# Beginning the row loads of two granules earlier in a fused attention and MLP kernel

## The chip, the cores and the metric

The kernel runs on one core of a Trainium2 chip. The metric is the device time of one execution, in microseconds (us). A trace gives a span that is some 1.8 us shorter, from the first to the last instruction on the engines. Ratios are the mean time of one kernel's fast runs over that of the other's fast runs of the same rounds, so they are not quite the ratio of the medians quoted beside them. The interval after a ratio is the 95% one.

## The reference, cut to what matters

```python
# attention: 4 batches, 8 heads, 768 positions, head size 64
scores = scale * q @ k^T + bias              # 8 global keys, 96 local keys, slopes by head
x = softmax(scores) @ v                      # then (3072 tokens, 512)
# MLP
h = x @ w_in                                 # 512 -> 2048
g = s * relu(h)**2 + b
out = g @ w_out                              # 2048 -> 512
```

## The kernel before

The 3072 tokens are cut into twelve granules of 256. A granule's k, q and v rows are loaded by GpSimd's DMA queue, which also casts them to bf16. Its k and q are transposed by DMA on SyncE's queue, its attention is computed, the result `xn` is transposed to `xT` by DMA (from granule 4 on), and the MLP follows one granule behind.

The parts that matter here:

```python
def load_granule(j):                 # six DMAs of 128 KB
    load_rows(j, "k"); load_rows(j, "q"); load_v(j)

def pace(j):                         # a one-element copy: GpSimd waits here for t
    t = pts[j, 0][0:1, 0, 0:1] if j < 5 else xT[j - 1][0:1, KC - 1, GT - 1 : GT]
    nc.gpsimd.tensor_copy(pdum[:], t)

def XT_dma(j):                       # two transposes by DMA, SyncE's queue
    xT[j] = xpool.tile([P, KC, GT], BF16, name="xT", tag="xT")
    for i in range(GB):
        nc.sync.dma_start_transpose(xT[j][:, :, i * P : (i + 1) * P], ...xn[j][:, i]...)

def idle(n, tag="pso", cols=4 * P):  # warm-up matmuls on constants
    ...
idle(9, "av")                        # the first work of the TensorE

def period(j, items, at, late=None, mid=()):      # granules 3 and 4
    SS(j, (0, 1))                    # scores, exp, mask product of two head pairs
    if j + 2 < NJ:
        pace(j)
        load_granule(j + 2)          # granules 5 and 6
    ...
    A(j, 0) ; A(j, 1, "psh")
    SS(j, (2, 3))
    A(j, 2) ; KO(j + 1) ; A(j, 3, "psh")   # KO, VO: VectorE copies of k and v
    if late is None:
        XT_dma(j)
    VO(j + 1)
    XB(j + 2)                        # transposes of k and q by DMA
    ...
# granules 5 to 11 (steady): the first product with w_in needs xT of the granule before
```

## Time and profile before

| | before |
|---|---|
| median of 3 runs | 209.95 us (209.49 to 210.19) |
| TensorE busy | 199.7 of 207.9 us |
| TensorE wait for xT of granule 4 | 0.57 us, at 79.36 |
| xT transposes of granule 4, issue to landing | 4.9 and 4.1 us |
| pacing copies for granules 5 and 6 | 54.80 and 66.40 us |

The TensorE's program order fixes what can be won: only where it waits. "SPq" in the views is SyncE's sequencer, which issues a transpose; "x2" is the number of instructions merged in a line; the bracket at the end of a line gives the idle time ahead of it and what ended it.

### The profile page before, as it was taken

To read this page: it belongs to the slowest core of one execution; us is meant where nothing else is said; L and a number is where in the kernel's file an instruction comes from. 1 tells how busy PE (TensorE), PEld (TensorE's weight loads), DVE (VectorE), ACT (ScalarE), POOL (GpSimd) and SP (SyncE) were. 2 spreads that over 40 slices of the span, in tenths; PEclk is the share of its full clock that TensorE was granted. 3 is DMA by queue.
4 is the path that set the end of the run, shared out by engine and by line. 5 is a ranking of instruction groups with operands and counts; after the bars stand their busy time and mean duration, and the time that the engine had idled before them with its cause. 6 is when DMAs were issued, how large, how long until landed. Compare 5 with 4: busy or idle time off the path is not lost.

```text
span 207.9 us, 5589 instructions
## 1 busy us (share of the span) xinstructions
PE 199.7 (96%) x2283; PEld 160.6 (77%) x2292; DVE 166.5 (80%) x401; ACT 120.2 (58%) x184; POOL 74.2 (36%) x98
## 2 busy tenths in 40 slices
PE   7989999999999998999999999999999999999992
PEld 2567976457666777888888988988988988988881
DVE  3575567599889898788799799788799799886682
ACT  5679899445978784636536536536446456425300
POOL 8985673930372806509119109027000000000000
PEclk9999999999999999999999999999999999999999
DMA  6999999999899995999999999969946040040022
GB/s 164 193 183 197 190 196 191 181 144 158 90 121 122 256 161 83 182 120 139 205 113 99 214 98 114 207 101 123 197 79 176 3 151 4 1 151 3 0 106 101
DMA packets 103850, 27.64 MB, mean 133 GB/s; under 512 B 91408, under 2 KB 101904, under 8 KB 103824
## 3 DMA queue, kind: packets, MB, share of 16 engines
q0 software_dynamic: 70976, 13.11, 80.2%
q1 hardware_dynamic: 31792, 13.64, 34.5%
q10 hardware_dynamic: 1056, 0.52, 0.9%
q8 instruction: 18, 0.29, 0.6%
q14 instruction: 8, 0.07, 0.2%
HBM read 27.26 MB, written 6.29 MB: 161 GB/s over the span
## 4 chain that ended last, share of the span: by engine, by line
PE 82%; ACT 9%; DMA 4%; DVE 2%; issue 1%; SPq 0%; ACTq 0%
PE ps L529 36%; PE ps_w L691 15%; PE ps_wb L691 7%; PE ps L590 6%; PE ps_av L447 5%; PE ps_s L396 4%; PE ps_wa L691 3%; ACT pt L409 3%; ACT gT L539 2%; DMA xT<-xn 2%; DMA raw<-in_k_dram 2%; PE ps_2s L590 2%; PE ps_s L380 1%; ACT gT L547 1%; ACT tmpl L256 1%
## 5 line engine op out<-in xcount | busy, mean ns | idle before, releaser
L529 PE MATMUL ps<-xT,w_in_bf 128*128 128x256 bf16 x768 | 96.7, 273 | 1.2 <-DMA xT<-xn 0.6
L529 PEld LDWEIGHTS <-w_in_bf 128*128 128x128 bf16 x768 | 72.8, 98 | 12.4 <-issue 0.9
L541 ACT ACTIVATE gT<-ps 128x512 bf16<-128x512 f32 x72 | 43.0, 598 | 58.7 <-PE ps L529 56.1
L409 ACT ACTIVATE pt<-ps_s 128x1024 bf16<-128x1024 f32 (+1 forms) x48 | 43.0, 951 | 2.7 <-PE ps_s L396 2.6
L691 PEld LDWEIGHTS <-sw 128*128 128x128 bf16 x288 | 28.1, 98 | 3.4
L419 DVE TENSOR_TENSOR pt<-pt,tmpl 128x1024 bf16<-128x1024 bf16 (+1 forms) x40 | 25.2, 648 | 3.0 <-ACT pt L409 2.4
L557 DVE TENSOR_TENSOR gT<-gT 128x512 bf16<-128x512 bf16 x66 | 25.1, 416 | 1.8 <-ACT gT L541 1.6
L691 PEld LDWEIGHTS <-gT 128*128 128x128 bf16 x216 | 20.5, 98 | 3.3 <-issue 0.2
L112 POOL DMA_DIRECT2D vaug<-in_v_dram x24 | 21.5, 912 | 4.2 <-DMA w_out_bf<-in_moe_w_out_dram 1.7
L465 DVE TENSOR_TENSOR xn<-ps_av,rc 128x256 bf16<-128x256 f32 x48 | 20.4, 425 | 1.7
L590 PE MATMUL ps<-w_out_bf,gT 128*128 128x512 bf16 x74 | 18.8, 379 | 0.5 <-issue 0.3
L126 POOL COPY pdum<-xT 1x1 bf16<-1x1 bf16 x5 | 3.8, 758 | 42.0 <-DMA xT<-xn 42.0
L691 PE MATMUL ps_w<-tw,sw 128*128 128x256 bf16 x144 | 18.7, 272 | 0.0
L701 DVE SCALAR_TENSOR_TENSOR u<-ps_w,s_bc,bvec 128x256 f32<-128x256 f32 x27 | 13.0, 480 | 6.7 <-PE ps_w L691 6.7
L447 PEld LDWEIGHTS <-pt 128*128 128x128 bf16 x352 | 15.5, 98 | 3.4 <-DVE xn L465 1.0
L104 POOL DMA_DIRECT2D qnat<-in_q_dram x18 | 16.0, 905 | 2.7 <-PE ps L529 1.4
L447 PE MATMUL ps_av<-vaug,pt 128*128 128x65 bf16 x224 | 16.4, 193 | 0.5 <-DVE xn L465 0.2
L539 ACT ACTIVATE gT<-ps 128x512 bf16<-128x512 f32 x24 | 14.2, 598 | 4.4 <-PE ps L529 4.4
L464 DVE RECIPROCAL rc<-ps_av 128x4 f32<-128x4 f32 x48 | 8.6, 179 | 10.2 <-PE ps_av L447 10.0
L104 POOL DMA_DIRECT2D knat<-in_k_dram x18 | 15.8, 887 | 1.6 <-issue 1.6
L590 PEld LDWEIGHTS <-gT 128*128 128x128 bf16 x96 | 8.6, 98 | 8.2
L396 PE MATMUL ps_s<-qT,kT 64*128 64x128 bf16 x224 | 12.3, 218 | 0.0
(94 smaller groups left out, 238.6 us busy)
## 6 DMA issues: line engine op xcount, KB each, us to landing
out_dram<-o_pr SPq DMA_DIRECT2D x8, 512.0 KB, 4.3
vaug<-in_v_dram POOLq DMA_DIRECT2D x24, 128.0 KB, 7.3
knat<-in_k_dram POOLq DMA_DIRECT2D x22, 128.0 KB, 5.2
qnat<-in_q_dram POOLq DMA_DIRECT2D x22, 128.0 KB, 6.5
w_in_bf<-in_moe_w_in_dram POOLq DMA_DIRECT2D x8, 256.0 KB, 8.3
w_out_bf<-in_moe_w_out_dram POOLq DMA_DIRECT2D x4, 512.0 KB, 10.0
out_dram<-o_pr SPq DMA_DIRECT2D x7, 256.0 KB, 4.0
raw<-in_q_dram ACTq DMA_DIRECT2D x2, 256.0 KB, 5.0
```

Of the source, the lines that this page charges most:

```text
L104: nc.gpsimd.dma_start(t[:, i, :, :], src[b, :, sb * P : (sb + 1) * P, :].rearrange("h p d -> p h d"))
L112: nc.gpsimd.dma_start(vaug[b % 2][:, sb, :, 0:D], v[b, :, sb * P : (sb + 1) * P, :].rearrange("h p d -> p h d"),)
L396: nc.tensor.matmul(ps[:, hi, oc * P : (oc + 1) * P], lhsT=kt[r, :], rhs=qT[j][r, hp, i * P : (i + 1) * P], start=not biased, stop=not bias ...
L409: nc.scalar.activation(pt[:, :, 0:n], ps[:, :, 0:n], ACT.Exp, scale=QSCALE)
L419: nc.vector.tensor_tensor(pt[:, :, 0:n], pt[:, :, 0:n], m, ALU.mult)
L447: nc.tensor.matmul(av[:, i, hi, :], lhsT=pt[:, hi, c * P : (c + 1) * P], rhs=vv, start=n_ == 0, stop=n_ == len(ops) - 1,)
L465: nc.vector.tensor_tensor(xn[j][:, :, 2 * hp : 2 * hp + 2, :], av[:, :, :, 0:D], rc[:].to_broadcast((P, GB, 2, D)), ALU.mult,)
L529: nc.tensor.matmul(ps[:, i, :], lhsT=w_in_bf[:, kc, fc * P : (fc + 1) * P], rhs=xT[j][:, kc, :], start=(kc == 0), stop=(kc == KC - 1),)
L541: nc.scalar.activation(gs.rearrange("p f (r t) -> p f r t", r=2), ps[:].rearrange("p f (t r) -> p f r t", r=2), ACT.Relu,)
L557: nc.vector.tensor_tensor(gs, gs, gs, ALU.mult)
L590: nc.tensor.matmul(po[j, tb], lhsT=gT[j][:, fc, tb * P : (tb + 1) * P], rhs=w_out_bf[:, fc, :], start=(fc == 0), stop=(fc == FC - 1),)
L691: nc.tensor.matmul(wt[j, ps], lhsT=lhs[:, f, :], rhs=rhs[:, f, :], start=first and f == 0, stop=f == HF - 1, skip_group_check=True,)
```

## The change

The intent is to fill a hole in the DMA traffic and get the rows out of the way of later transposes. Granule 5's load moves to the first evacuated output of granule 1, granule 6's to granule 3's third exp.

```diff
-    def pace(j):
-        t = pts[j, 0][0:1, 0, 0:1] if j < 5 else xT[j - 1][0:1, KC - 1, GT - 1 : GT]
+    def pace(t):
         nc.gpsimd.tensor_copy(pdum[:], t)
...
     P2_raw(1, 0)
+    pace(raw[1, 0][0:1, 0:1])
+    load_granule(5)
...
     def period(j, items, at, late=None, mid=()):
         SS(j, (0, 1))
-        if j + 2 < NJ:
-            pace(j)
-            load_granule(j + 2)
...
         SS(j, (2, 3))
+        if j == 3:
+            pace(pts[j, 2][0:1, 0, 0:1])
+            load_granule(6)
...
-            pace(j)
+            pace(xT[j - 1][0:1, KC - 1, GT - 1 : GT])       # granules 7 to 11: as before
             load_granule(j + 2)
```

## The prediction

> **What bounds the kernel now.** I read four views: the engines' busy shares, the waits of the TensorE, the timelines of the three engines around the moved loads, and the DMA share in one-microsecond windows. The busy shares come first, because they say how much there is to win at all.
>
> ```profile
> span 207.9 us, 5589 instructions
> PE 199.7 (96%) x2283; PEld 160.6 (77%) x2292; DVE 166.5 (80%) x401; ACT 120.2 (58%) x184; POOL 74.2 (36%) x98
> ```
>
> The TensorE is busy for 199.7 of 207.9 us, at a granted clock of 1.000 throughout. The loads themselves are on no engine that is full: GpSimd, which issues them, is at 36%. So the change cannot save more than the TensorE waits that these loads cause, and the next view lists those:
>
> ```profile
> PE ps_i L239 <- PEq L1134: 0.8, 1, 0.8
> PE ps L529 <- DMA xT<-xn: 0.6, 1, 0.6
> PE ps_t L272 <- ACT knat L160: 0.6, 1, 0.6
> PE ps L590 <- issue: 0.3, 2, 0.2
> ```
>
> The columns are total us, times, longest. Only the second line is a wait for a transfer: once in the whole run, 0.6 us long, for a transpose by DMA of the attention output. The first and third lie in the first six microseconds, before anything that is changed. The timeline of the TensorE places it:
>
> ```profile
> 78.33 1.03 PE L691 MATMUL ps_wa<-w_out_bf,gT 128*128 128x256 bf16 x8
> 79.93 1.92 PE L529 MATMUL ps<-xT,w_in_bf 128*128 128x256 bf16 x16 [0.57 <-DMA xT<-xn]
> ```
>
> The product of granule 4 with w_in waits until 79.93 for xT of granule 4, 0.57 us after the TensorE had finished its earlier work at 79.36. The SyncE timeline shows when that transpose was issued, and the GpSimd timeline what stood ahead of it:
>
> ```profile
> 47.30 3.15 SPq L321 DMA_TRANSPOSE kT<-knat  x2
> 50.64 2.50 SPq L329 DMA_TRANSPOSE qT<-qnat  x2
> 58.97 3.31 SPq L321 DMA_TRANSPOSE kT<-knat  x2
> 62.45 2.50 SPq L329 DMA_TRANSPOSE qT<-qnat  x2
> ...
> 74.52 2.50 SPq L508 DMA_TRANSPOSE xT<-xn  x2
> ```
>
> ```profile
> 43.85 0.88 POOL L112 DMA_DIRECT2D vaug<-in_v_dram  x1 [1.11 <-DMA qnat<-in_q_dram]
> 54.80 0.18 POOL L126 COPY pdum<-pt 1x1 bf16<-1x1 bf16 x1 [10.07 <-DVE pt L419]
> 55.70 1.75 POOL L104 DMA_DIRECT2D knat<-in_k_dram  x2 [0.72 <-issue]
> ...
> 66.40 0.51 POOL L126 COPY pdum<-pt 1x1 bf16<-1x1 bf16 x1 [5.43 <-DVE pt L419]
> 66.85 1.75 POOL L104 DMA_DIRECT2D knat<-in_k_dram  x2
> 68.58 1.77 POOL L104 DMA_DIRECT2D qnat<-in_q_dram  x2
> 70.32 1.78 POOL L112 DMA_DIRECT2D vaug<-in_v_dram  x2
> ```
>
> The rows of granule 6 are issued from 66.85 to 72.1. Their last transfers take 6.2 us from issue to landing by the DMA view of that window, so they are in flight until about 71.2 + 6.2 = 77.4. The two transposes of xT, issued at 74.5 and 75.8, share the DMA engines with that tail and take 4.9 and 4.1 us. The same pair two granules later, at 104 and 105, takes 3.6 and 2.8 us. On the other side, the DMA engines had a hole shortly before (the last two columns are the DMA share and GB/s):
>
> ```profile
> 55.00:56.00 1.00, 1.00 (x16) 0.92 (x14) 0.91 (x3) 0.97 (x3) 0.30 (x1) 1.00 0.07 8
> 56.00:57.00 1.00, 0.91 (x21) 0.76 (x20) 0.55 (x3) 1.00 (x2) 1.00 (x2) 1.00 0.00 0
> ```
>
> The hole is the pacing copy at 54.80: GpSimd waited 10.07 us for it while the earlier queue drained.
>
> **What the Trainium skill says.** In "DMA: Bandwidth & Descriptors", section "Queues, rings and completion order", each DMA engine goes round-robin between the queue rows with work, packet by packet. The transposes (SyncE's queue) and the row loads (GpSimd's queue) therefore share an engine rather than stand behind one another. The trace agrees: transposes of k issued beside queued loads at 37.2 landed after 7.7 us, those issued to a quiet queue at 80 after 2.4 us. Section "Issuing engines are not separate DMA queues" says that starting from another engine buys no bandwidth; only the time of the load counts here. In "SBUF — State Buffer", section "SBUF: two separate sides", VectorE instructions in a two-port mode can lock GpSimd out of a shared port while it writes descriptors. The trace shows only a small sign of such a conflict: the copy of ko at 60.62, beside GpSimd's issue of v, took 0.60 us, that at 73.27, with GpSimd idle, 0.42. Load issues stay at 0.88 us each beside a busy VectorE.
>
> **The change part by part.** It neither adds nor removes work. The order of instructions, compared before and after, is the same on all five engines; only what the two one-element copies read differs, and with that their time.
>
> Granule 5. The copy waited for the mask product of granule 3's first exp (54.80). Now it waits for granule 1's first evacuated output, the third ScalarE instruction of that kind, at 46.90 with 0.69 us, so 47.6. The issues run from about 48.0 (copy 0.2, then a start) to 53.3 (six by 0.88). The waits on earlier landings don't hold them much: the slots free when rows of granule 3 and 4 land, the latest of them needed being the second q load of granule 4 at about 41 + 10.2 = 51.2, just when the second v issue comes up. The k slot also waits for granule 3's k transposes, landed by 38.7 + 8.1 = 46.8. So the move is about 7.7 us. But the queue still holds granule 4's v until 43.85 + 9.5 = 53.4, so the data flow from about 53.4 instead of 57: they fill the hole, some 3 to 4 us earlier.
>
> Granule 6. The copy waited for granule 4's first exp product (66.40). Now it waits for granule 3's third. These two products run together, 58.41 to 59.67, so the third is ready at about 59.0. Issues run from 59.3 to 64.6 instead of 66.85 to 72.1, 7.5 us earlier.
>
> When do the DMA engines drain? An estimate: one granule's rows are six of 128 KB, 0.79 MB, at the 155 GB/s seen in the windows 73 to 76 about 5.1 us. From 53.4 on there are 3.4 us of granule 4's transposes, 5.1 of granule 5's rows, about 3 of its transposes, 2.6 for four output stores of 256 KB at the 400 GB/s seen at 68 to 69, and 5.1 of granule 6's rows: 19.2 in all, so empty at about 72.6 instead of 77.4. That is about 2 us before the transposes of xT at 74.52. They then run alone and should take 2.8 to 3.6 us: the second lands near 75.8 + 3.0 = 78.8, ahead of 79.36.
>
> Sum on the path: minus 0.57 us, all of the one wait. It passes on whole, if the VectorE is ready 0.57 us sooner for what follows. Attention for granule 5 would start at 81.12; its product with the mask is done at 79.36 (78.68 + 0.68). The next head pair at 82.2 needs 80.95. Both hold. From 85 to the end the TensorE runs with hardly a gap (5.00 of 5 in each window from 80 to 95), so a start 0.57 us sooner ends 0.57 sooner. I take off 0.05 for small effects: 209.95 - 0.52 = 209.43, called 209.4.
>
> **The rivals.** First: a new wait at granule 4's transposes. Granule 5's rows now compete with the k and q transposes issued at 47.3 to 53.1, which landed at 53.5 to 56.8 with the queue to themselves at the end. The 3.4 us left at 53.4 might double, to 60.2. They are needed by the ko copy at 60.62 and by the score matmuls at 63.60. The first has only 0.4 us to spare if it were the q transposes, but it needs k alone, due by about 57. So I expect no wait; if it came, up to 1 us, which gives 210.4.
>
> Second: the VectorE. It is busy without a gap from 41.84 to 55.4, and granule 3's attention matmuls at 55.07 stand 0.27 us behind its products. GpSimd's issues move beside that stretch, and granule 6's beside the ko and vo copies at 60.62 to 62.8. If each of a few copies lost the 0.18 us seen once, 0.2 to 0.5 us would be lost on the VectorE, and of that perhaps 0.2 on the TensorE. That gives 209.6. Against it: the tensor-tensor products beside load issues at 68 to 72 took 0.69, as they do without.
>
> Third: hidden anyway. If the drain takes longer than estimated (small packets share badly: 160 GB/s at best), the tail still meets xT and the wait shrinks to half. That gives 209.7. Nothing at all would be 209.95.
>
> Fourth: more than the wait. Granule 7's load is paced by xT of granule 4 and starts about 1 us sooner, but no TensorE wait for a transfer is left there to remove. I see no way to gain over 1 us.
>
> **Range and chances.** The three runs before span 0.7 us, 209.49 to 210.19, and a median of three may sit 0.2 off. With the gain between 0 and 0.6 in most cases and a loss of up to 0.3 in some, eight times in ten I expect 209.0 to 210.1. 2% is 4.2 us, far more than all waits concerned, so 98% for within 2%, and 1% for each side.
>
> **What would show it.** Right: the wait for xT gone from the TensorE's list, no DMA hole at 55 to 57, copies at about 48 and 59, xT transposes at about 74.5 landing in 2.7 to 3.6 us, and a span near 207.4. Wrong: a new TensorE or VectorE wait for kT or qT of granule 4 at 60 to 64; mask products or copies lengthened between 48 and 65; or xT still above 4 us because the queue drains later than 74.

## The result

The changed kernel took 209.92 us (median of 4 runs, 209.64 to 210.01), the kernel before 210.03 in the same rounds. The ratio is 0.9997 (0.9976 to 1.0018): the same. The granted clock of 0.997 in some runs, of both kernels, is no part of the story: in the changed kernel's trace it falls only after 206 us, when the TensorE has finished.

Everything that the prediction said of the loads happened. These are the pacing copies in GpSimd's timeline of the changed kernel:

```profile
47.60 0.35 POOL L125 CAST pdum<-o_pr 1x1 bf16<-1x1 f32 x1 [2.98 <-ACT o_pr L622]
...
59.06 0.60 POOL L125 COPY pdum<-pt 1x1 bf16<-1x1 bf16 x1 [5.20 <-DVE pt L418]
```

They stand at 47.6 and 59.1, 7.2 and 7.3 us earlier. In the one-microsecond windows the hole at 55 to 57 is filled, and the DMA engines are idle just before the xT transposes (the last two columns are DMA share and GB/s):

```profile
55.00:56.00 1.00, 1.00 (x16) 0.91 (x15) 0.88 (x3) 0.97 (x3) 0.00 (x0) 1.00 2.07 166
56.00:57.00 1.00, 0.86 (x21) 0.72 (x19) 0.55 (x3) 0.97 (x3) 0.00 (x0) 1.00 3.08 84
...
74.00:75.00 1.00, 1.00 (x11) 0.89 (x10) 0.93 (x4) 0.40 (x1) 0.00 (x0) 1.00 0.00 0
```

And yet the TensorE waits as before. Its timeline, and the chain of waits around it:

```profile
78.39 1.03 PE L690 MATMUL ps_wa<-w_out_bf,gT 128*128 128x256 bf16 x8
80.04 1.92 PE L528 MATMUL ps<-xT,w_in_bf 128*128 128x256 bf16 x16 [0.62 <-DMA xT<-xn]
```

```profile
75.06 0.72 SPq L507
75.78 0.05 issue
75.83 4.17 DMA xT<-xn
80.00 0.05 issue
```

The second transpose of xT still takes 4.17 us, beside 2.4 us for the first. So what slowed it was not the rows. The DMA view of the window from 77 to 78, in which the data of the second transpose move, shows something that the prediction had not looked for:

```profile
q1 hardware_dynamic: 498, 0.12, 164.0%
q8 instruction: 1, 0.02, 5.7%
issues: line engine op xcount, KB each, median us to landing
xT<-xn SPq DMA_TRANSPOSE x1, 4.2
```

The columns of a queue are packets, MB and the time of its packets. One packet of an instruction queue falls in that window. The kernel before has one in the same window. The table is from the packets' records in the two traces. The transposes' queue has packets of 256 bytes (median time 18 ns) and of 4 bytes.

```
                                  before             changed
row packets last seen             77.1               73.4
first transpose's data            75.75 to 77.2      75.75 to 76.6
instruction packet, 16 KB         77.24 (1.15 us)    77.57 (0.92 us)
transposes' queue, over 0.6 us,
  begun from 75.0 to 79.2         26                 24
  256 bytes, 4 bytes              15, 11             18, 6
both transposes' 1024 packets of
  256 bytes:
  begun by 78.0                   990                990
  the other 34                    78.3 to 78.9       78.4 to 78.9
first k transpose of granule 6    from about 79.0    from about 79.2
```

The two 990 say most: by 78.0 the transposes were equally far in both kernels, with the rows' tail and without it, and the last 34 packets began only when the instruction packet was about to end (at 78.39 and 78.49). 34 is about what one of the 16 DMA engines carries of a transpose (512 packets / 16 = 32), so my estimate is that one engine alone was late; the records don't name the engine.

There are 18 such 16 KB packets in a run of either kernel, and one comes every 246 recorded TensorE instructions on average (4532 less 351, over 17 gaps, in the kernel before; some matmul records are missing; single gaps are from 174 to 335). The Trainium skill, in "Runtime: NRT & Kernel Launch", section "Instruction fetch mechanics", says that an engine's instruction memory is refilled in blocks of 16 KiB, 256 instructions, by a DMA queue of the sequencer's own; "instruction packet", "instruction transfer" and "refill" mean the same below. The size and the mean spacing agree. It calls the cost mostly hidden; here the suspicion is that it slows a transpose that the TensorE waits for.

There is a small second difference. The vo copies of granule 4 on the VectorE, at 61.84 and 62.63 in the changed kernel, take 0.76 and 0.83 us instead of 0.43 each, as GpSimd now issues granule 6's loads beside them.

### The profile page after: what moved, and what is told of

Its sections match the earlier page's. It is cut to its first block, busy times and chain, and to the rows that moved or that the text cites. A ratio compares the mean times of both kernels' runs of the same rounds, so it can differ in the third digit from the quotient of the medians.

```text
span 208.2 us, 5598 instructions
## 1 busy us (share of the span) xinstructions
PE 200.8 (96%) x2292; PEld 160.7 (77%) x2292; DVE 167.1 (80%) x401; ACT 120.2 (58%) x184; POOL 74.5 (36%) x98
## 4 chain that ended last, share of the span: by engine, by line
PE 79%; ACT 9%; DVE 4%; DMA 4%; issue 2%; SPq 0%; ACTq 0%; DVEq 0%
PE ps L528 35%; PE ps_w L690 14%; PE ps_wb L690 6%; PE ps L589 6%; PE ps_av L446 5%; PE ps_s L395 4%; ACT pt L408 3%; PE ps_wa L690 3%; ACT gT L538 2%; DMA xT<-xn 2%; DMA raw<-in_k_dram 2%; PE ps_2s L589 2%; PE ps_s L379 2%; DVE xn L464 1%; ACT gT L546 1%
## 5 line engine op out<-in xcount | busy, mean ns | idle before, releaser
L540 ACT ACTIVATE gT<-ps 128x512 bf16<-128x512 f32 x72 | 43.0, 598 | 59.1 <-PE ps L528 56.3
L589 PE MATMUL ps<-w_out_bf,gT 128*128 128x512 bf16 x80 | 19.7, 379 | 0.0
```

Of the source, the lines that this page charges most:

```text
L540: nc.scalar.activation(gs.rearrange("p f (r t) -> p f r t", r=2), ps[:].rearrange("p f (t r) -> p f r t", r=2), ACT.Relu,)
L589: nc.tensor.matmul(po[j, tb], lhsT=gT[j][:, fc, tb * P : (tb + 1) * P], rhs=w_out_bf[:, fc, :], start=(fc == 0), stop=(fc == FC - 1),)
```

## The experiments

Theory A: the TensorE's instruction transfer at about 77.5 slows the second xT transpose, and the rows' tail made no wait. The rival is the prediction's own: the rows' tail makes the wait. A test must move one without the other. The instruction transfers follow the count of TensorE instructions, so cutting the warm-up matmuls at the start into more, smaller ones moves all transfers earlier and is meant to leave the rest as it was. Results were correct in all runs. e1 to e4 and p1 to p4 are single runs: their traces are read, but their times (208.79 to 211.01 us without p4, beside 210.63 and 209.63 for the kernel before) are not ranked.

### e1: the changed kernel, transfers moved by 126 instructions

```diff
-    idle(9, "av")
+    idle(72, "av", 64)
```

> The changed kernel with its nine warm-up matmuls of 512 columns cut into seventy-two of 64 columns: the same columns, 126 more TensorE instructions, so each 16 KB instruction transfer of the DMA's instruction queue should come some 6 us earlier (near 71 to 72 instead of 77.57). Theory A (the second xT transpose of granule 4 is slowed by the instruction transfer beside it): that transpose lands in under 3.2 us instead of 4.2, the TensorE's wait for xT (0.62) is gone (under 0.15), the span is near 207.6. Theory B (the transposes of that time are slow for another reason, such as their own pairing or the k transposes behind them): the wait stays at 0.5 to 0.7.

The warm-up took 4.00 us, as before. The nearest instruction packets now began at 72.60 and 83.55. The transposes landed after 2.4 and 2.5 us, and the TensorE waited for nothing:

```profile
78.71 1.03 PE L690 MATMUL ps_wa<-w_out_bf,gT 128*128 128x256 bf16 x8
79.58 1.91 PE L528 MATMUL ps<-xT,w_in_bf 128*128 128x256 bf16 x16
```

The bracket is gone, the span is 207.5 us. Theory A said under 3.2 us to landing and no wait.

### e2: the kernel before, the same warm-up

The edit is the same. This is the run that should tell the theories apart, as the rows' tail is still there.

> The kernel before with the same cut warm-up, so granule 6's rows still end near 77.3. Theory of the prediction (the tail of the row loads is what slows xT): the wait of 0.57 stays, 0.4 to 0.6. Theory A (the instruction transfer does): the first transpose is still slowed by the tail (near 4.9 us to landing), but the second lands by about 78.9, and the wait is gone or under 0.15. If both are needed, the wait is halved, near 0.3.

The transposes took 3.4 and 2.6 us to land, the TensorE's list of waits has no xT, the span was 207.2 us:

```profile
78.41 1.03 PE L691 MATMUL ps_wa<-w_out_bf,gT 128*128 128x256 bf16 x8
79.28 1.91 PE L529 MATMUL ps<-xT,w_in_bf 128*128 128x256 bf16 x16
```

So the tail does slow the first transpose (by about 1 us against e1), but within slack. The first transpose's 4.9 us, expected to stay, did not: in the kernel before its 512 packets were through by 77.31, but it landed at 79.38, so the instruction packet held it too.

The tail did not stay quite as it was. Its last packet came at 77.0 as before, but only 127 row packets began after 75.5, where the kernel before has 1128; in t2, the same kernel again, there were 654, the last at 77.5, the second transpose landed at 79.08, and there was no wait either. By itself e2 is therefore weaker than planned. The rival falls by this with the rest: the changed kernel has no tail and the full wait, and in the kernel before 990 of the 1024 packets had begun by 78.0 in spite of the tail.

### e3: the changed kernel, transfers moved by a whole period

```diff
-    idle(9, "av")
+    idle(137, "av", 34)
```

> The changed kernel with the warm-up cut into 137 matmuls of 34 columns: 256 more TensorE instructions, a whole instruction transfer's worth, so that the transfers fall where they fell, with one more of them in all. Theory A: a transfer at 77 to 78 again and the wait for xT is back, 0.4 to 0.8. If it is the mere number of short warm-up matmuls that took the wait away in the run before, it is under 0.15 here too.

256 more instructions put a transfer back: there is one at 78.73 in a run that is some 1.1 us late by an early wait of its start phase, and 19 in all. The wait is back too:

```profile
PE ps L528 <- DMA xT<-xn: 0.6, 1, 0.6
```

The transposes took 2.4 and 4.2 us, as in the changed kernel. So it is neither the small matmuls nor their number, but where the transfer falls.

### p3: a small dose, 18 instructions

```diff
-    idle(9, "av")
+    idle(18, "av", 256)
```

> A small dose: the changed kernel with the warm-up cut into eighteen matmuls of 256 columns, 18 more TensorE instructions, so the instruction transfer comes 0.8 to 1 us earlier, at about 76.7, between the two transposes' data (75.75 to 76.5 and from 77.0). Theory A: it still runs into the second transpose's first half, so the wait shrinks, to 0 to 0.4, and the second transpose lands in 3 to 4 us. If the coincidence did not matter, the wait stays at 0.6.

The transfer moved further than expected, to 75.36, onto the first transpose. The transposes took 3.8 and 3.3 us to land, neither enough for a wait, and the span was 207.0 us. The expected position was a miss; why it moved by 2.2 us instead of 0.9 is not shown, but single gaps between transfers differ by much more than 18 instructions in every run, so the count of instructions does not fix the place closely. That the wait goes when the transfer leaves the second transpose fits.

### p1 and p2: each part alone

p1 moves only granule 6, p2 only granule 5:

```diff
# p1, against the changed kernel         # p2, against the changed kernel
-    pace(raw[1, 0][0:1, 0:1])           -        if j == 3:
-    load_granule(5)                     -            pace(pts[j, 2][0:1, 0, 0:1])
+    # in period(3), after SS(3, (0, 1)): -            load_granule(6)
+        pace(pts[3, 0][0:1, 0, 0:1])    +    # in period(4), after SS(4, (0, 1)):
+        load_granule(5)                 +        pace(pts[4, 0][0:1, 0, 0:1])
                                         +        load_granule(6)
```

> One part alone: granule 6's loads at granule 3's third exp, granule 5's at granule 3's first exp as before. The two loads follow one another at about 55.7 and 61, the DMA engines still have their hole at 55 to 57 and are drained by about 75. The instruction transfer still falls on the second xT transpose: wait 0.5 to 0.8. GpSimd issues granule 6's rows beside the vo copies, so these are long again (over 0.7 us each).

> The other part alone: granule 5's loads at granule 1's first evacuated output, granule 6's at granule 4's first exp as before. No hole at 55 to 57; ko and vo copies of granule 4 at 0.42 to 0.43 us, as GpSimd is idle there; granule 6's tail as before, the first xT transpose near 4.9 us to landing; wait for xT 0.5 to 0.7 by the instruction transfer.

In both a 16 KB instruction packet began at 77.7 to 77.8, the second transpose took 4.2 us and the first 2.4, and the wait for xT was 0.6. So neither part alone, nor both, touches it. In p1 one ko copy (0.60) and one vo copy (0.85) were long, the other vo copy not (0.43), so "both over 0.7" was half missed; its last row packet came at 76.1, not by about 75. In p2 the copies took 0.42 and 0.43 as expected, but the first transpose did not take 4.9 us: with granule 5 out of the way early, granule 6's rows, though paced as before, were nearly through when it started.

### e4: granule 6 paced by the vo copy

```diff
-        if j == 3:
-            pace(pts[j, 2][0:1, 0, 0:1])
-            load_granule(6)
...
             VO(j + 1)
+        if j == 3:
+            pace(vos[4][0:1, GB - 1, H - 1, 0:1])
+            load_granule(6)
```

> The changed kernel with granule 6's loads paced by granule 4's finished vo copy (about 62.7) instead of granule 3's third exp (59.1). If GpSimd's load issues are what lengthened the VectorE's ko and vo copies (vo 0.76 and 0.83 us instead of 0.43 and 0.43), they are back at 0.42 to 0.45, the first mask product of granule 4 starts near 65.6 instead of 66.09, and the TensorE is some 0.1 us ahead of the changed kernel at 80. The wait for xT stays (0.5 to 0.8) under theory A. Rival: the copies are slowed by the DMA traffic, and stay long.

VectorE's timeline in the changed kernel and then in e4:

```profile
61.84 0.76 DVE L353 COPY vo<-vaug 128x1040 bf16<-128x1040 bf16 x1
62.63 0.83 DVE L356 COPY vo<-vaug 8x1040 bf16<-8x1040 bf16 x1
```

```profile
61.67 0.43 DVE L353 COPY vo<-vaug 128x1040 bf16<-128x1040 bf16 x1
62.14 0.43 DVE L356 COPY vo<-vaug 8x1040 bf16<-8x1040 bf16 x1
```

The DMA engines were busy with granule 5 in both, only GpSimd's issues were gone from beside the copies, so it is the issues that lengthen them. The Trainium skill describes such a conflict in "SBUF — State Buffer", section "Who interferes with whom": copies in a two-port mode and GpSimd block each other; that these copies are in such a mode no run shows. It says that tensor-tensor products have no two-port mode and, with both inputs in SBUF, contend only with GpSimd's reads, and infers that issuing a load needs the write side; those beside load issues kept their 0.69 us, which agrees. On the path it is worth little: the matmuls that follow the wait for xT begin at 79.96 in e4 and 80.04 in the changed kernel. The wait stayed, 0.64 us, with a transfer at 77.49.

### p4: granule 6 late, no transfer near

```diff
-        if j == 3:
+        if j == 4:
             pace(pts[j, 2][0:1, 0, 0:1])
             load_granule(6)
...
-    idle(9, "av")
+    idle(72, "av", 64)
```

> The small warm-up (72 matmuls of 64 columns) with granule 5 early, but granule 6's loads paced still later than before, by granule 4's third exp product (about 71.8), so that all its rows meet the xT transposes of granule 4. If the prediction's model holds at all (rows beside the transposes delay them), the transposes take 4.5 to 6 us to land and the TensorE waits 0.5 to 2 us for xT, though no instruction transfer is near. If rows never matter there: no wait, and under 3.9 us to landing.

It asks whether rows can hurt at all. They can: the transposes took 6.4 and 7.5 us (4.5 to 6 expected), the TensorE waited 4.17 us for xT, twice the most that was expected, and its granted clock fell to 0.50 during that wait, at 82.7, until 89.5. Its timeline, and the windows (after the width of a window come the busy times of PE, PEld, DVE, ACT and POOL; the third number from the right is the granted clock):

```profile
84.45 3.60 PE L528 MATMUL ps<-xT,w_in_bf 128*128 128x256 bf16 x16 [4.17 <-DMA xT<-xn]
```

```profile
80.00:84.00 4.00, 0.28 (x3) 0.00 (x0) 2.85 (x6) 0.11 (x1) 0.00 (x0) 0.84 2.38 132
84.00:86.00 2.00, 1.54 (x8) 1.12 (x9) 0.00 (x0) 0.00 (x0) 1.11 (x3) 0.50 1.32 192
```

Sixteen matmuls that take 1.92 us in the changed kernel took 3.60 at a clock of 0.50. The whole run took 216.57 us, 6.9 more than the kernel before on the same chip; about 1 us of that is an early wait of its start phase for k rows. The nearest instruction packets were at 70.78 and 89.10. So the prediction's mechanism exists; in the kernel before the rows were early enough not to trigger it (in e2 and t2 the second transpose landed 0.9 and 0.2 us before the TensorE came to it).

### t1 to t4: timed, five rounds on one chip

t1 is the changed kernel again, t2 the kernel of e2, t3 that of e1, and t4 that of e4 with the warm-up of e1.

> The changed kernel as it is, timed again beside the kernel before. Its wait for xT is as long as before (0.62 against 0.57), and the VectorE's longer copies cost some 0.1 us: ratio 1.000 to 1.001.

> The kernel before with the warm-up cut into 72 matmuls of 64 columns, timed. Theory A (instruction transfer): the xT wait of 0.57 is gone, ratio 0.997 (0.6 us less) if nothing else changes. The one profile so far showed 207.2 us of span, 0.7 less than before. If the wait was only hidden elsewhere: ratio 1.000.

> The changed kernel with that warm-up, timed. If earlier row loads bring nothing once the instruction transfer is out of the way, it is no faster than the kernel before with the same warm-up, by 0 to 0.3 us slower: ratio 0.997 to 0.999. If the row loads' tail does cost time there, it is faster than that one, ratio under 0.996.

> Both mends: granule 6 paced by granule 4's vo copy, and the small warm-up. No wait for xT (under 0.15), copies of vo back at 0.43 us, span near 207.3, ratio 0.996 to 0.998. It should be 0.1 to 0.3 us faster than the changed kernel with the small warm-up alone, and equal to the kernel before with it.

| kernel | median us | ratio to before | TensorE wait for xT in its trace |
|---|---|---|---|
| before, same rounds | 210.03 | | 0.57 (first trace) |
| t1 changed | 210.19 | 1.0010 (0.9993 to 1.0027) | 0.68 |
| t2 before, small warm-up | 208.99 | 0.9950 (0.9936 to 0.9965) | none |
| t3 changed, small warm-up | 208.96 | 0.9952 (0.9935 to 0.9969) | none |
| t4 vo-paced, small warm-up | 208.96 | 0.9947 (0.9931 to 0.9963) | none |

One run of the kernel before took 520.47 us; it counts as slow and is left out of the ratios. With the transfer moved, the kernel before gains 1.0 us, and moving the rows adds nothing to it: t2, t3 and t4 lie within 0.03 us. The copies that t4 mends cost nothing measurable either; its expected 0.1 to 0.3 us over t3 is a miss. t2 to t4 are the fastest of the versions timed, and the plain warm-up edit is all that they need. All three gained more than was expected (ratios of 0.996 to 0.999): t3's 0.9952, under the 0.996 named as a sign that the tail costs time, is no such sign, as t2, with a tail, has 0.9950.

The gain of 1.0 us is more than the wait of 0.57. Part of the reason is in how the wait is shown. These are the two matmul groups in t2:

```profile
78.42 1.03 PE L691 MATMUL ps_wa<-w_out_bf,gT 128*128 128x256 bf16 x8
79.29 1.91 PE L529 MATMUL ps<-xT,w_in_bf 128*128 128x256 bf16 x16
```

Without a wait the second group starts 0.87 us after the first, while the first is still shown as running. In the kernel before it starts 79.93 - 78.33 = 1.60 us after it, in the changed kernel 1.65. So the wait shown as 0.57 costs 1.60 - 0.87 = 0.73 us. Aligning the weight loads of the two traces from their ends, t2 is 0.10 us behind the kernel before after the start phase, 0.65 ahead after 79.9 and 0.74 ahead at the end, with a step of 0.1 at 155.4.

That step is a second case of the same, and one without rows. In the kernel before, the second xT transpose of granule 9 is issued at 151.16; an instruction packet begins at 153.27, no row packet falls between its issue and its landing, and it takes 4.12 us to land. The product that needs it starts 0.97 us after the group ahead of it:

```profile
154.45 1.05 PE L691 MATMUL ps_w<-w_out_bf,gT 128*128 128x256 bf16 x8
155.42 1.03 PE L529 MATMUL ps<-xT,w_in_bf 128*128 128x256 bf16 x8
```

In t2, without an instruction packet there, the transpose takes 2.47 us and the product starts 0.88 us after the group ahead. Over the kept traces in which no row packet is beside this transpose: with an instruction packet 2.1 us after the issue 4.12, 4.29 and 4.20 us (before, changed, t1), without one 2.46 to 2.47 us (e1, e2, t2, t3, t4, p4).

The first trace of the kernel before was also a short one: 207.9 us, where the ten fast runs beside t2 had spans of 207.7 to 208.8. So some 0.3 us of the gain between the medians is not placed.

## Why the prediction was right or wrong

The range and the class held: 209.92 lies between 209.0 and 210.1. The point of 209.4 and its reason did not: the range held only because it had left room for no gain at all.

- What moves when: right. Copies at 47.6 and 59.1 (said: 47.6 and about 59.0), the hole filled.
- When the DMA engines drain: right. Said about 72.6, seen 73.4 for the last row packet, with nothing moving from 74 to 75.
- "They then run alone and should take 2.8 to 3.6 us": this is the step that failed. They ran free of rows, but the second did not run alone: it took 4.17 us beside an instruction packet. The trace of the kernel before had that packet, in its queue list and in the window 77 to 78; I had named the tail of the rows as the cause because the two overlapped, and compared with the pair at 104 us without asking what else differed.
- "Minus 0.57 us, all of the one wait": nothing of it came; the wait measured 0.62 and 0.68 in the changed kernel's two traces. The wait itself could be had, as e1 and t2 show, by other means, and passed on whole to the end; it was under-sized, 0.73 us instead of 0.57, as a matmul's shown end overlaps the next one's start.
- First rival, a new wait at granule 4's transposes: none came. The q transposes took up to 8.9 us to land instead of about 5, and still made it.
- Second rival, the VectorE: its mechanism came, more strongly than said (0.3 to 0.4 us on each vo copy instead of 0.18), but on the TensorE it was worth 0.1 at most.
- Third rival, hidden anyway: closest in outcome (it gave 209.95 for "nothing at all"), but for another cause than the slow drain that it named. Its "160 GB/s at best" was a misreading: in the kernel before, 404 transposes' packets of 256 bytes or less moved 0.10 MB in the 0.5 us from 65.0, some 200 GB/s.
- Two small misreadings changed nothing: the pair at 104 us took 3.6 and 2.7 us (said: 2.8), and granule 4's transposes in the kernel before had landed by 56.4 (said: 56.8).

What is not settled is why one 16 KB packet holds up the 34 packets, about one DMA engine's share, for over a microsecond, some of them past its own end. Nor does every slow packet come from it: of the transposes' queue's packets over 0.6 us, 88 of 93 overlap an instruction packet in the changed kernel, but 102 of 145 in the kernel before and 24 of 111 in t2.

## What to carry to other kernels

Before moving a load to free a transfer, list everything that is on the DMA engines while that transfer is under way, the instruction queues included; the largest neighbour in bytes was not the one that set its end. A wait of half a microsecond at one place can depend on where the refill of the TensorE's instructions falls, and then any edit that adds or removes TensorE instructions ahead of it can shift the time by half a per cent, as the 72 small warm-up matmuls did here; a shift by a number of instructions that costs no time, and a control by one whole period, tell this apart from the edit's own effect. Earlier loads bring nothing where the rows already arrive within slack, but rows that are late enough stall the TensorE; in p4 the granted clock fell as well, which cost some 2.5 us on top of the wait of 4.2 (from the first matmul after the wait to the return of the clock, p4 falls from 4.87 to 7.33 us behind e1).

## What the Trainium skill lacked or had wrong

- "Runtime: NRT & Kernel Launch", section "Instruction fetch mechanics", calls the cost of a refill mostly hidden. Here the TensorE's refill beside a DMA transpose lengthened that transpose from 2.5 to 4.2 us and cost the TensorE 0.6 us; moving all refills by 126 instructions gave a ratio of 0.9950.
- "DMA: Bandwidth & Descriptors" describes packet-wise sharing in "Queues, rings and completion order", but not that one instruction packet can hold back a DMA transpose far beyond its share of bandwidth: beside one 16 KB packet of 0.92 us, 18 packets of 256 bytes, where the median is 18 ns, and 6 of 4 bytes took over 0.6 us each, and the transpose took 1.7 us longer to land than in e1.
- "SBUF — State Buffer", section "Who interferes with whom", names one slowdown of VectorE (6.8 times) without the instructions, and none for copies beside GpSimd's load issues: here a bf16 copy of 1040 columns went from 0.43 to 0.76 and 0.83 us.
